# An exception path behind a flag: which block stands in front of the end, who issues its transfers, and a branch hint

## The chip, the cores and the metric

The kernel runs on one core of a Trainium2 chip. The metric is the device time of one execution in microseconds.

## What is computed

Multi-head attention, its heads put side by side, then a two-layer network with a SiLU gate. In and out are float32.

```python
# q, k, v: (8, 12, 448, 64); w_in: (768, 2048); w_out: (2048, 768)
scores = q @ k.transpose(0, 1, 3, 2) / np.sqrt(64)
scores = scores - scores.max(-1, keepdims=True)
attn = np.exp(scores)
attn = attn / (attn.sum(-1, keepdims=True) + 1e-9)
x = (attn @ v).transpose(0, 2, 1, 3).reshape(3584, 768)
h = x @ w_in
out = (h * (1.0 / (1.0 + np.exp(-h)))) @ w_out
```

## The kernel before

The program has two paths that compute the same thing. The first, `without_maximum`, leaves out the subtraction of the row maximum. It is right as long as the sums of the exponentials stay within bounds. The second, `with_maximum`, is a plain, slow version with the maximum; it is there for inputs on which the first path is not accurate, and with the inputs measured here it does not run.

**First path.** Work on attention is cut into 24 units (8 batches, 3 groups of 4 heads). GpSimd issues the loads; TensorE makes the scores, ScalarE their exponentials, VectorE the sums' inverses and the scaling; the results go to the first layer as 16-bit tiles. The second layer is computed in fast products (sums and differences of blocks, called `S` and `D`, in place of some multiplications): `product` makes them on TensorE, `take`, `add_in`, `add_out` and `take_out` bring them out of PSUM through ScalarE and VectorE into `ost` tiles, and `store` sends those to the output from SP, near the end from ScalarE too. The last product is made in two column halves (L966, 16 matmuls of 192 columns for the second). `take_half` (L1033 to L1040) copies them out, one half on VectorE (L1039), the other on ScalarE (L1037), and `store_last` issues one store of 96 KB for each (L1004), from SP and from ScalarE.

**The order** of all instructions is made by a planner: the class `Order` keeps a model time for each engine, and every operation is noted in `od.out` with the model time at which it starts. At the end the list is sorted by that time and written out, so each engine's queue follows it. `od.pe_last` is the model time at which TensorE's last operation starts.

**The flag.** `judge` (L213) runs in three steps placed some time after the last inverse sum: GpSimd compares all inverse sums with two bounds, VectorE and a small transfer reduce the answers to one number, and GpSimd writes it as an integer to `flag` (L232): 1 if the first path was good. `read_flag` (L1921) has each of the five engines load `flag` into a register with a TENSOR_LOAD (L1922). It is placed at `od.pe_last`, so behind most of the work in each queue.

**The branch.** `tc.If(fine != 1, preferred_fallthrough_block=False)` at L210 is carried out by each engine for itself, when its own queue comes to it. The argument says that the false side follows directly on the branch. There is no `Else`, so the false side holds only what the framework puts there: waits and additions that bring the semaphores to the values that they would have after the other side. In memory the order of the code is: first path, false side, true side (`with_maximum`), end block. The end block (its instructions have the line of the launch, L1956) holds SP's waits on all transfers and engines and then a barrier of the five engines. In `with_maximum` every transfer is issued by SP: the second layer's weights once, and in loops over batches and heads the loads of `q`, `k` and `v`, four small transfers of row maxima a head, the first layer's weights and the output. The arithmetic there is on TensorE, VectorE and ScalarE.

## Time and profile before

| | us |
|---|---|
| median of 3 runs | 387.40 (387.12 to 387.53) |
| the profiled execution | 386.63 |
| its span, first to last instruction | 384.84 |
| last matmul group (L966) starts | 374.13 |
| last copy (L1037) starts | 376.10, takes 0.32 |
| last store is issued (L1004, ScalarE) | 376.45 |
| granted TensorE clock | 0.995 |

In the profile's lines an engine's name with a q behind it (SPq, ACTq) is that engine's sequencer: its DMA issues, branches, semaphore waits and register loads, which are not counted as busy. PEldq stands for TensorE's sequencer. A line with "x2: 38/46/53, 376.7 to 380.3" gives how often an instruction ran, its shortest, median and longest duration in nanoseconds, and when the first and the last started. An instruction's duration does not include the time after it in which the engine has no instruction to run; that shows as the distance to the next one.

### The profile page before, as it was taken

The page shows a single profiled execution, that of the slowest core. Times are in us where ns is not written, and L with a number is a line of the kernel's source. Part 1 is how long each engine was busy: PE and PEld are TensorE (multiplying, and loading weights), DVE is VectorE, ACT ScalarE, POOL GpSimd, SP SyncE. Part 2 cuts the span into 40 slices and gives each one's busy share as a digit, 9 for nine tenths or more (in the row PEclk, how much of TensorE's full clock was granted, in tenths as well). Part 3 has the DMA queues.
Part 4 walks back from the last instruction along what each step waited for, and adds up shares of the span by engine and source line. Part 5 has one row for each costly group of instructions (what it writes and reads, how often), then busy time and mean ns, then how long its engine had stood idle before and what let it go on. Part 6 is the DMA issues. An engine that isn't in the chain of part 4 may idle for free. (4 is left out here: it accounts for less than half of the span.)

```text
span 384.8 us, 12974 instructions
## 1 busy us (share of the span) xinstructions
PE 374.1 (97%) x5516; PEld 192.6 (50%) x5516; DVE 280.8 (73%) x562; ACT 257.7 (67%) x425; POOL 91.1 (24%) x160
## 2 busy tenths in 40 slices
PE   8999999999999999999999999999999999999990
PEld 7433455444545444544444554555556555556660
DVE  5779799999978779996879897899784345473420
ACT  4998845887867787868697877558752288862220
POOL 7538517206051605142411400030020000000000
PEclk9999999999999999999999999999999999999997
DMA  7999999847367824558661712110003320002331
GB/s 116 202 204 195 189 210 193 123 87 105 64 111 145 139 43 50 82 93 157 97 115 27 97 40 68 34 33 1 2 20 84 92 52 2 1 22 67 99 97 55
DMA packets 36001, 34.74 MB, mean 90 GB/s; under 512 B 12000, under 2 KB 35168, under 8 KB 35936
## 3 DMA queue, kind: packets, MB, share of 16 engines
q0 software_dynamic: 25232, 22.82, 39.7%
q1 hardware_dynamic: 10176, 10.53, 10.2%
q8 instruction: 45, 0.74, 0.7%
q10 hardware_dynamic: 528, 0.49, 0.5%
q14 instruction: 20, 0.16, 0.1%
HBM read 45.61 MB, written 11.01 MB: 147 GB/s over the span
## 5 line engine op out<-in xcount | busy, mean ns | idle before, releaser
L608 ACT ACTIVATE E<-banks 128x896 f16<-128x896 f32 x168 | 144.0, 920 | 40.7 <-PE banks L570 40.4
L560 PE MATMUL banks<-xT,w_in_t 128*32 128x448 f16 (+1 forms) x1446 | 90.5, 353 | 0.0
L560 PE MATMUL banks<-w_out_t,G 128*32 128x384 f16 (+1 forms) x968 | 67.4, 327 | 0.0
L560 PEld LDWEIGHTS <-G 128*32 128x32 f16 (+1 forms) x1240 | 46.9, 97 | 34.0 <-issue 6.5
L560 PEld LDWEIGHTS <-w_in_t 128*32 128x32 f16 (+1 forms) x1446 | 42.2, 97 | 43.3 <-issue 12.7
L506 POOL DMA_DIRECT2D V<-in_v_dram x84 | 46.0, 555 | 57.2 <-PE banks L645 42.9
L570 PE MATMUL banks<-rq,KT 32*128 32x448 f16 (+1 forms) x768 | 52.1, 362 | 0.3 <-ACT E L608 0.2
L769 ACT ACTIVATE th<-banks 128x448 f16<-128x448 f32 x72 | 37.2, 553 | 15.0 <-PE banks L560 12.3
L807 DVE SCALAR_TENSOR_TENSOR G<-th,banks 128x448 f16<-128x448 f16 (+1 forms) x72 | 39.9, 573 | 4.8 <-ACT th L769 4.5
L1030 ACT COPY ost<-banks 128x384 f32<-128x384 f32 x41 | 19.8, 486 | 33.0 <-PE banks L560 21.4
L560 PE MATMUL banks<-D,S 128*32 128x384 f16 (+1 forms) x544 | 38.1, 327 | 0.0
L929 ACT ACTIVATE G<-banks 128x448 f16<-128x448 f32 (+3 forms) x72 | 33.8, 554 | 5.3 <-DVE banks L912 3.5
L645 PE MATMUL banks<-E,V 128*32 128x448 f16 x672 | 35.7, 353 | 0.0
L743 DVE SCALAR_TENSOR_TENSOR xT<-banks,rdn 128x448 f16<-128x448 f32 x48 | 29.2, 618 | 5.6 <-PE banks L645 3.0
L912 DVE TENSOR_TENSOR banks<-banks,q 128x448 f32<-128x448 f32 x28 | 17.6, 632 | 15.7 <-PE banks L896 14.5
L560 PEld LDWEIGHTS <-S 128*32 128x32 f16 (+1 forms) x544 | 20.6, 97 | 14.7 <-issue 3.1
L619 DVE TENSOR_TENSOR T<-E,E 128x1792 f16<-128x1792 f16 x22 | 23.8, 1081 | 5.7 <-ACT E L608 5.5
L483 POOL DMA_DIRECT2D rq<-in_q_dram x25 | 13.9, 555 | 58.4 <-PE banks L570 47.8
L619 DVE TENSOR_TENSOR T<-T,E 128x1792 f16<-128x1792 f16 x22 | 23.9, 1086 | 5.2 <-ACT E L608 5.1
L570 PEld LDWEIGHTS <-KT 32*128 32x128 f16 (+1 forms) x768 | 12.3, 96 | 29.6 <-issue 26.9
L645 PEld LDWEIGHTS <-V 128*32 128x32 f16 x672 | 17.0, 97 | 16.0 <-issue 3.9
L896 PEld LDWEIGHTS <-w_in_t 128*128 128x128 f16 x168 | 16.4, 98 | 15.2
(163 smaller groups left out, 409.4 us busy)
## 6 DMA issues: line engine op xcount, KB each, us to landing
out_dram<-ost SPq DMA_DIRECT2D x200, 48.0 KB, 1.6
rk<-in_k_dram POOLq DMA_DIRECT2D x23, 224.0 KB, 5.2
rq<-in_q_dram POOLq DMA_DIRECT2D x23, 224.0 KB, 5.1
w_out_t<-in_moe_w_out_dram POOLq DMA_DIRECT2D x4, 768.0 KB, 13.4
V<-in_v_dram POOLq DMA_DIRECT2D x42, 64.0 KB, 3.6
V<-in_v_dram POOLq DMA_DIRECT2D x42, 48.0 KB, 4.2
w_in_t<-in_moe_w_in_dram POOLq DMA_DIRECT2D x3, 512.0 KB, 10.4
w_in_t<-in_moe_w_in_dram POOLq DMA_DIRECT2D x6, 256.0 KB, 6.1
```

Source lines behind the costliest of these rows:

```text
L506: nc.gpsimd.dma_start(out=v_of(b, hg0)[32 * x : 32 * (x + 1), at, 0:count, :], in_=v[b, hs].rearrange("h (i g) d -> i h g d", g=TPP)[:, :, ...
L560: nc.tensor.matmul(out=out[at], lhsT=lhsT[:, at], rhs=rhs, **flags)
L570: nc.tensor.matmul(out=pS[p0 : p0 + 32 * (x1 - x0), h % 2, at : at + nq], lhsT=KT[(b, hg)][32 * h : 32 * (h + 1), c, x0:x1, :, e], rhs=QT[ ...
L608: nc.scalar.activation(out=E[(n, w)][0:kr, 2 * y : 2 * y + 2, 0:nk], in_=pS_t[(n, w, y)][0:kr, :, 0:nk], func=AF.Exp, scale=attn_scale,)
L619: nc.vector.tensor_tensor(out=T[n], in0=T[n] if step else E[(n, 0)], in1=E[(n, step + 1)], op=ALU.add,)
L645: nc.tensor.matmul(out=a[32 * h : 32 * (h + 1), 0:nq], lhsT=w, rhs=e[k0:k1, h, at : at + nq], start=start, stop=stop,)
L743: nc.vector.scalar_tensor_tensor(out=x3(b, cc)[:, cc % 3, 32 * g0 : 32 * g1], in0=acc[(n, part)][:, 0:nq], scalar=0.5, in1=rdn_t[n].rearra ...
L769: nc.scalar.activation(out=th, in_=h_t[(b, f, t0)][:, 0 : t1 - t0], func=AF.Tanh)
L807: nc.vector.scalar_tensor_tensor(out=dst[:, f, at + lo : at + hi], in0=th_t[(b, f, t0)][:, lo - t0 : hi - t0], scalar=1.0, in1=h_t[(b, f, ...
L912: nc.vector.tensor_tensor(out=pp_t[(f, to)], in0=pp_t[(f, x)], in1=pf_t[(f, y)], op=ALU.add)
L929: nc.scalar.activation(out=o, in_=a, func=AF.Silu, scale=2.0)
L1030: nc.scalar.copy(out=ost(qd, i, j), in_=bank(qd, m))
```

## The change

The second path's transfers are issued by GpSimd in place of SP. The flag is inverted: 0 now means that the first path was good. `with_maximum` moves from the true side of the branch to an `Else`; the true side, taken when the flag is 0, is empty. `preferred_fallthrough_block=False` stays, so the code of the false side follows on the branch and the empty true side comes behind it, in front of the end block. A new step `foretell`, placed 5 us of model time ahead of `od.pe_last`, has ScalarE, VectorE, GpSimd and SP load the flag once more and give a hint, from that register, on the branch labelled "judged". TensorE has no hint. The later load of the flag, on which the branch decides, stays where it was.

```diff
-    fine = without_maximum(tc, q, k, v, moe_w_in, moe_w_out, out, guard, flag)
-    with tc.If(fine != 1, preferred_fallthrough_block=False):
+    ran_over = without_maximum(tc, q, k, v, moe_w_in, moe_w_out, out, guard, flag)
+    with tc.If(ran_over == 0, preferred_fallthrough_block=False, label="judged") as answer:
+        pass
+    with answer.Else():
         with_maximum(tc, q, k, v, moe_w_in, moe_w_out, out)
...
-        nc.gpsimd.tensor_copy(out=flag, in_=one)
+        nc.gpsimd.tensor_scalar(
+            out=flag, in0=one, scalar1=-1.0, scalar2=1.0, op0=ALU.mult, op1=ALU.add
+        )
...
-    nc.sync.dma_start(out=w_out_t, in_=moe_w_out.rearrange("(f p) m -> p f m", p=128))
+    nc.gpsimd.dma_start(out=w_out_t, in_=moe_w_out.rearrange("(f p) m -> p f m", p=128))
...
-        nc.sync.dma_start(out=raw, in_=src[b, h].rearrange("(g i) d -> i g d", i=32))
+        nc.gpsimd.dma_start(out=raw, in_=src[b, h].rearrange("(g i) d -> i g d", i=32))
...
-            nc.sync.dma_start(out=vt, in_=v[b, h].rearrange("(c p) d -> p c d", p=112))
+            nc.gpsimd.dma_start(out=vt, in_=v[b, h].rearrange("(c p) d -> p c d", p=112))
...
-                nc.sync.dma_start(out=row[:, 112 * c : 112 * (c + 1)], in_=m)
+                nc.gpsimd.dma_start(out=row[:, 112 * c : 112 * (c + 1)], in_=m)
...
-            nc.sync.dma_start(
+            nc.gpsimd.dma_start(
                 out=w,
...
-            nc.sync.dma_start(out=out[at : at + 112], in_=o)
+            nc.gpsimd.dma_start(out=out[at : at + 112], in_=o)
...
+    def foretell():
+        some = [ENG.Activation, ENG.DVE, ENG.Pool, ENG.SP]
+        guess = nc.values_load(flag, engines=some, skip_runtime_bounds_check_because=why)
+        tc.mark_branch_hint_location("judged", guess, some)
+
+    od.out.append((od.pe_last - 5.0, len(od.out), foretell))
     od.out.append((od.pe_last, len(od.out), read_flag))
```

## The prediction

> **What bounds the kernel now.** I read the page first: where the span goes, and what is left of it when the arithmetic is over.

> ```profile
> span 384.8 us, 12974 instructions
> ...
> PE 374.1 (97%) x5516; PEld 192.6 (50%) x5516; DVE 280.8 (73%) x562; ACT 257.7 (67%) x425; POOL 91.1 (24%) x160
> ...
> PE   8999999999999999999999999999999999999990
> ```

> TensorE is busy to the last slice, and that slice is empty. The change touches nothing that feeds TensorE, so the question is the last slice. The timeline of its last ten microseconds comes next:

> ```profile
> 374.13 1.48 PE L966 MATMUL banks<-D,G 128*128 128x192 f16 x16
> ...
> 376.10 0.32 ACT L1037 COPY ost<-banks 128x192 f32<-128x192 f32 x1 [1.29 <-DVE ost L1039]
> 376.45 0.65 ACTq L1004 DMA_DIRECT2D out_dram<-ost  x1
> ```

> The last instruction that computes ends at 376.4 us and the last store is issued at 376.45; the span runs to 384.8. So 8.4 us are left with no arithmetic. What fills them are branch and semaphore instructions, which the views by source line show: line 210 (the `tc.If`) and line 1956 (the end of the program). Columns: operation, count, shortest/median/longest in ns, first and last start.

> ```profile
> L210 SPq EVENT_SEMAPHORE  x8: 17/17/17, 376.8 to 380.2; - x8
> L210 POOLq COMPARE_BRANCH  x2: 38/39/40, 287.6 to 287.7; - x2
> L210 PEldq COMPARE_BRANCH  x2: 90/2132/4173, 374.4 to 375.8; - x2
> L210 DVEq COMPARE_BRANCH  x2: 51/53/55, 375.7 to 376.2; - x2
> L210 SPq COMPARE_BRANCH  x2: 38/46/53, 376.7 to 380.3; - x2
> L210 ACTq COMPARE_BRANCH  x2: 38/50/61, 377.1 to 377.3; - x2
> ```
> ```profile
> L1956 SPq EVENT_SEMAPHORE  x14: 17/28/28, 383.2 to 384.8; - x14
> ...
> L1956 POOLq DRAIN  x3: 46/107/5792, 287.9 to 384.6; - x3
> L1956 SPq DRAIN  x3: 7/7/7, 384.0 to 384.3; - x3
> L1956 DVEq DRAIN  x2: 10/45/80, 379.3 to 384.3; - x2
> L1956 ACTq DRAIN  x2: 8/44/81, 379.9 to 384.3; - x2
> L1956 PEldq DRAIN  x2: 8/40/73, 380.0 to 384.3; - x2
> ```

> Each engine branches twice. The first branch (not taken: the flag is 1) falls into an empty block that only settles semaphores; the second jumps over all of `with_maximum` to the end block. From second branch to first instruction of the end block: DVE 376.2 to 379.3, 3.1 us; ACT 377.3 to 379.9, 2.6; PE 375.8 to 380.0, 4.2; SP 380.3 to 383.2, 2.9; POOL 287.7 to 287.9, 0.2. POOL is the control: in the code every transfer of `with_maximum` is SP's and its arithmetic is on the other three, so POOL has next to nothing to jump over. A long jump costs 2.6 to 4.2 us, a short one 0.2. Four of the five are covered, because SP still waits for the stores; SP's is not. It stands behind its eight waits of line 210, whose last are for the two output halves; issued at 376.1 and 376.45, these take 3.7 and 3.5 us and so land by 380.0. In the windows nothing else runs:

> ```profile
> 378.70:380.00 1.30, 0.00 (x0) 0.00 (x0) 0.00 (x0) 0.00 (x0) 0.00 (x0) 1.00 0.06 15
> ...
> 380.30:383.20 2.90, 0.00 (x0) 0.00 (x0) 0.00 (x0) 0.00 (x0) 0.00 (x0) 0.62 0.04 11
> ```

> The last two columns are the DMA share and GB/s. From 378.7 to 380.0 the share is 0.06, one engine of sixteen, with the last of the output on it. The DMA view from 375 to 380 names who else was there:

> ```profile
> q14 instruction: 3, 0.02, 1.6%
> q8 instruction: 1, 0.02, 1.5%
> ```

> One instruction packet of 16 KB took 1.5% of 16 x 5 us, 1.2 us on a single engine, just while the output was being written; the output packets of that engine came after it. Code is being loaded for the jumps, and it delays the landing.

> **The change part by part, on the profiled execution (386.63 us: span 384.84 and 1.79 around it; the median of the runs, 387.40, is 0.77 higher).**

> *Order of the blocks.* The false side is still the one that falls through, but it is now `with_maximum`; the true side, empty, comes behind it and runs into the end block. So each engine jumps once, at its first branch. For SP that is at 376.7, right behind its last store, in place of 380.3: the jump leaves the path behind the landing, **-2.9 us**. It lies beside the landing, which lasts to 380.0; even a full 2.9 us from 376.7 would end at 379.6.

> *Transfers from GpSimd.* SP keeps next to nothing in `with_maximum`, so its jump should cost what POOL's did, 0.2. The transfer queues of SP are also no longer used by the second path, so the empty block need not level their semaphores: the eight waits of line 210 go. Three of them stood behind the landing (the rows of SP at 380.0 to 380.3), **-0.3**. POOL gets the long jump: it branches at 287.6, 96 us before anyone asks for it; covered.

> *The end block's waits.* SP has twelve waits from 383.2 to 384.0, 0.065 us each; with the narrower window eight start by 383.64, and four and a drain follow from 383.7. The two halves' semaphores stand at the eighth and ninth. Arriving early, SP has done the first seven before the landing: 383.2 to 383.7, **-0.5**. What stays behind the landing is 383.7 to 384.84, 1.1 us.

> *The landing itself.* PE's jump, not hinted, now starts at 374.4 in place of 375.8, 1.4 us earlier; at the row's 4.2 us it is done by 378.6, and its 16 KB packet ends at about 377.3 in place of 378.7. Behind it that DMA engine has its sixteenth of the 192 KB store (the window 376.5 to 377.0 moved 0.17 MB, so 0.57 us) and of the two halves (378.7 to 379.6 before, 0.9). That gives 378.8 for the last packet where it was 379.6: **-0.8**. The bounds are 0 (another packet in the way) and -1.4 (all of the shift). The hinted engines' packets move to about 370, out of this stretch.

> *Loading the flag early and the hint.* On ACT, DVE, POOL and SP one TENSOR_LOAD, 0.48, 0.54, 0.50 and 0.97 us by the rows of line 1922, and a hint, which no row shows. Queued behind them on ACT are the copies that empty the last banks, on DVE the additions of line 1043, on SP the stores. Five microseconds ahead of the last product is about 369: there ACT idles 0.92 and 1.70 us before its copies, DVE 3.41 before line 1043, SP waits 2.7 for the copy of 370.4. Loads on the sequencer also run beside an operation (DVE's at 373.05 beside the addition at 373.03). Taken as 0, with 0.1 left for the sum. Bounds of the hint: nothing, or the 2.6 to 3.1 us of a whole fetch if it holds its queue; less than nothing is excluded, since all that it could save is the jumps, priced already. Less those idle stretches the upper end is about 1.3 us on the last copies.

> *The inverted flag.* One GpSimd operation at 285 takes the place of another (1.99 us), 80 us ahead: 0.

> Sum: -2.9 - 0.3 - 0.5 - 0.8 + 0.1 = -4.4, so 386.63 becomes 382.2, and against the median 387.4 becomes **383.0 us**. Next late after the landing (379.2) is PE, out of its jump at 378.6.

> **Rivals.**

> *The landing does not come earlier.* Another engine's code packet, or PE's own, meets the halves again. For: four packets in five microseconds, on engines I cannot choose. Against: three of them should have gone by then. Price: the 0.8 returns, 383.8. Chance 0.22.

> *The hint fetches nothing.* DVE then starts its fetch at 375.7 and ACT at 377.1, as early or earlier than before, and both are out at 378.8 and 379.7, before or at the landing; SP's short jump is untouched. Their two packets stay in the output's stretch, so the 0.8 shrinks or goes: 383.5 to 384.0. Speaking for it is that no row shows a hint. [...] Chance 0.12.

> *Nothing moves.* If the block in front of the end still closes with a jump that is not local, or SP keeps code enough in the second path for a jump behind the landing, all of 2.9 + 0.3 + 0.5 comes back: 387.4. Against: the empty block is now the neighbour of the end. Chance 0.04.

> *Slower.* [...] Chance 0.06.

> **How the numbers follow.** Forecast 0.56, the others as above. A measurement of this kernel can tell about 0.2%, 0.8 us, from no change. The first three cases are faster by more: 0.90. Nothing moves: 0.04 same. Slower: 0.06. The range goes down to the whole shift of the landing and a little run spread (387.4 - 5.1 = 382.3, so 382.0) and up past both milder rivals and the hint's upper end (383.8 + 1.3 = 385.1, so 385.0). The likeliest case alone spans 382.2 to 383.6.

> **What would show it.** Right: one branch per engine of the `tc.If`; SP's at 376.7 with the end block's first wait within about 0.3 us; no semaphore waits of SP between; the last wait of the landing followed by the end after 1.1 us; landing near 379.2; span near 380.4. PE's branch should still show some 4 us. Wrong: SP's gap of 2.9 us still behind the landing; idle time before the copies of 370 to 376 grown by more than the loads; a last copy later than 376.1; or PE's jump ending after the landing, which would make PE the last to arrive.

## The result, and the profile after

The changed kernel takes 383.88 us (median of 4 runs, 383.29 to 383.98) against 387.46 us for the kernel before (4 runs): a ratio of 0.9905, 95% interval 0.9888 to 0.9922, 3.6 us less. Its profiled execution took 383.98 us with a span of 382.2.

The spans of the two profiled executions differ by 2.7 us only. All work up to the last store is 0.9 us later in the one after (its last store is issued at 377.38, that of before at 376.45). We put that down to spread between executions and not to the change: the profiled execution of before was 0.8 us under its median, and in the profiles of the runs below, apart from the one that moves that store to SP, it is issued anywhere from 376.6 to 377.5. From the issue of the last store to the end of the span the two show 384.84 - 376.45 = 8.4 us and 382.18 - 377.38 = 4.8 us, and this difference of 3.6 us is the one of the medians. In what follows, times of the tail are counted from that issue.

The branch of the changed kernel (by source line: operation, count, shortest/median/longest ns, first and last start):

```profile
L210 PEldq COMPARE_BRANCH  x1: 3594/3594/3594, 375.4 to 375.4; - x1
L210 DVEq COMPARE_BRANCH  x1: 84/84/84, 376.7 to 376.7; - x1
L210 SPq COMPARE_BRANCH  x1: 64/64/64, 377.9 to 377.9; - x1
L210 ACTq COMPARE_BRANCH  x1: 76/76/76, 378.1 to 378.1; - x1
L210 PEldq EVENT_SEMAPHORE  x1: 51/51/51, 379.0 to 379.0; - x1
L210 DVEq EVENT_SEMAPHORE  x1: 21/21/21, 379.6 to 379.6; - x1
L210 ACTq EVENT_SEMAPHORE  x1: 17/17/17, 381.3 to 381.3; - x1
```

Each engine branches once, and SP's eight waits of this line are gone. But the long jumps are all still there: from branch to the next instruction PE 3.6 us (which its branch record itself lasts), DVE 2.9, ACT 3.2. The hints of ACT and DVE ran at 369.8 and 370.8, and no code was fetched for them: between 365 and 376 the DMA view lists no instruction packet at all. The end block and ScalarE's hint (a hint too has the line of the launch), and SP's own waits:

```profile
L1967 SPq EVENT_SEMAPHORE  x14: 17/28/28, 378.1 to 382.1; - x14
...
L1967 ACTq BRANCH_PREFETCH_HINT  x1: 54/54/54, 369.8 to 369.8; - x1
```
```profile
SPq L1967 <- ACTq L210: 1.5, 1, 1.5
SPq L1967 <- DMA out_dram<-ost: 1.1, 3, 0.4
```

SP enters the end block at 378.1, 0.2 us after its branch, in place of 383.2. It then waits 1.1 us for the output, and after that 1.5 us for ScalarE. Landing times of the last two stores (KB, us from issue):

```profile
out_dram<-ost SPq DMA_DIRECT2D x1, 96.0 KB, 2.3
out_dram<-ost ACTq DMA_DIRECT2D x1, 96.0 KB, 2.2
```

They were 3.7 and 3.5. The output is there at 379.6, when VectorE's jump ends too; after that only ScalarE's jump is outstanding, for another 1.7 us.

### The profile page after: what moved, and what is told of

Its sections match the earlier page's. It is cut to its first block, busy times and chain, and to the rows that moved or that the text cites. A ratio compares the mean times of both kernels' runs of the same rounds, so it can differ in the third digit from the quotient of the medians.

```text
span 382.2 us, 12974 instructions
## 1 busy us (share of the span) xinstructions
PE 374.5 (98%) x5516; PEld 192.9 (50%) x5516; DVE 280.9 (73%) x562; ACT 257.6 (67%) x425; POOL 91.1 (24%) x160
## 4 chain that ended last, share of the span: by engine, by line
PE 92%; ACT 2%; DMA 2%; POOL 1%; DVE 1%; issue 1%; POOLq 0%
PE banks L565 53%; PE banks L901 15%; PE banks L575 10%; PE banks L650 10%; ACT E L613 2%; DMA rq<-in_q_dram 2%; PE banks L971 2%; PE banks L666 2%; DMA out_dram<-ost 1%; POOL rk L480 0%; DVE T L624 0%; POOL rq L488 0%; PE banks L686 0%; DVE rq L558 0%; DVE ost L1053 0%
```

## Experiments

Ratios are to the kernel before on the same chip, with 95% intervals. Where source lines shift, the end block has another number (L1956, L1966 or L1967 in the lines shown).

**The hint taken away.**

```diff
-    od.out.append((od.pe_last - 5.0, len(od.out), foretell))
```

> The changed kernel without the early load and the hint. Theory (the hint fetched nothing: in the changed kernel ScalarE's jump still took 3.2 us and VectorE's 2.9): same time as the changed kernel, 383.9 us within 0.5, with ScalarE's end-block entry again the last to arrive, some 3.9 us after the last store is issued. Rival (the hint did part of the work, for instance kept the output's landing at 2.2 us): the landing goes back to 3.5 us and the time up by about 1 us.

Measured: 384.14 us, ratio 0.992 (0.9897 to 0.9942); it and the changed kernel's interval overlap over more than half of each.

```profile
L210 ACTq COMPARE_BRANCH  x1: 62/62/62, 377.6 to 377.6; - x1
L210 ACTq EVENT_SEMAPHORE  x1: 17/17/17, 380.4 to 380.4; - x1
```

ScalarE's jump takes 2.8 us without a hint and 3.2 with it, and is the last arrival in both; the landing is 2.5 us without the hint. At 5 us ahead the load and the hint gain nothing that can be measured.

**Transfers alone.** The kernel before, with only the second path's transfers moved from SP to GpSimd; its lines are numbered as before.

> The kernel before with the second path's transfers on GpSimd; order of the blocks and flag as before. Theory: SP's jump behind the landing is then local (0.2 us in place of 2.9) and its eight waits are gone; ScalarE's second branch starts 0.85 us after the last store and takes 2.6 to 3.2, so it is last: 383.6 to 384.2, nearly all of the gain without the change of order. Rival (the gain comes from the order of the blocks): 386.5 to 387.4.

Measured: 383.75 us, ratio 0.9902 (0.9885 to 0.9918), the whole gain.

```profile
L210 SPq COMPARE_BRANCH  x2: 38/46/53, 377.0 to 377.1; - x2
L210 ACTq COMPARE_BRANCH  x2: 38/50/61, 377.5 to 377.7; - x2
```
```profile
q8 instruction: 1, 0.02, 1.5%
out_dram<-ost ACTq DMA_DIRECT2D x1, 96.0 KB, 3.6
```

SP has no second jump behind the landing, nor waits between its two branches. Here TensorE still jumps late (376.2), a packet of 16 KB lies in the output (377.8; that it is TensorE's, the run without its code shows below), and the landing takes 3.6 us, beside 3.5 in the kernel before. It ends at 380.4, where ScalarE (380.5) and TensorE (380.5) come out of their jumps too. So the earlier jumps of the changed kernel bring the landing forward (2.2 us), and ScalarE's jump (3.2 us) uses that up.

**Order of the blocks alone.** The changed kernel without the hint, its second path's transfers back on SP.

> The changed kernel without the hint and with the second path's transfers back on SP: only the order of the blocks and the flag are changed. Theory: SP jumps right behind its last store, 2.9 us beside the landing, and then has its eight waits (0.5) and the twelve of the end block (0.8) to do, which the changed kernel did during the landing: SP becomes last instead of ScalarE, about 0.8 us behind it, 384.7 us; most of the gain of 3.6 is there. Rival (the gain comes from SP having no code to jump over): no gain, 387.4.

Measured: 385.1 us, ratio 0.9938 (0.9922 to 0.9955), 2.6 us gained.

```profile
L210 SPq EVENT_SEMAPHORE  x8: 17/17/17, 380.6 to 381.1; - x8
...
L210 SPq COMPARE_BRANCH  x1: 45/45/45, 377.4 to 377.4; - x1
```

SP's jump is long again, 3.2 us, but starts 0.8 us behind the last store, without waiting for the output. That output has landed at 379.2, so the jump lies beside the landing for 1.8 us and is the last thing for another 1.4. Then come the eight waits and the twelve of the end block (its drain is at 381.9), with SP still last. Either part alone thus ends the state in which SP begins its jump only when the output is there: the order lets the jump begin earlier, the transfers make it short. The gains do not add up, because both remove the same wait.

**A hint 75 us ahead**, in front of the last two code packets of queue q14 before the tail (334.3 and 351.1 us in the changed kernel).

```diff
-    od.out.append((od.pe_last - 5.0, len(od.out), foretell))
+    od.out.append((od.pe_last - 75.0, len(od.out), foretell))
```

> The changed kernel with the early load and the hint 75 us of model time ahead in place of 5, ahead of the last code packets that ScalarE and VectorE fetch in sequence (332 to 351 us). Theory A (a hint is only served together with a later fetch in sequence, so 5 us was too late): the jumps of ScalarE and VectorE shrink from 3 us to some tenths, the landing or TensorE's jump becomes last, and the time falls by about 1.5 us to 382.3. Theory B (the hint is not served in this program at any distance): 383.9, jumps of 3 us as before.

Measured: 382.81 us, ratio 0.9871 (0.9847 to 0.9894). Once more, on a chip with the changed kernel beside it:

> The hint 75 us ahead once more: 1.0 to 1.3 us below the changed kernel on the same chip (382.7), because ScalarE's jump is short and the landing and VectorE's jump, both some 2.3 us after the last store's issue, are last.

> The changed kernel once more, beside the next two on one chip: 383.9 us, a ratio of 0.990 to 0.991 to the kernel before; ScalarE's jump last, about 3.9 us after the last store's issue.

Measured there: 382.38 (382.28 to 382.84), ratio 0.9871 (0.9854 to 0.9888), against 383.10 (382.72 to 383.90), ratio 0.9892 (0.9873 to 0.9912), for the changed kernel. The step is 0.7 us, less than the 1.0 expected. The early hint came out 0.3 us under its 382.7, the changed kernel 0.8 under its 383.9. The two intervals overlap; of the runs only the slowest of the one and the fastest of the other cross. ScalarE's jump took 2.8 us in this profile of the changed kernel, 3.2 in the first. From the first run of the early hint:

```profile
L210 DVEq COMPARE_BRANCH  x1: 84/84/84, 376.7 to 376.7; - x1
...
L210 ACTq COMPARE_BRANCH  x1: 76/76/76, 378.1 to 378.1; - x1
L210 ACTq EVENT_SEMAPHORE  x1: 17/17/17, 378.6 to 378.6; - x1
...
L210 DVEq EVENT_SEMAPHORE  x1: 21/21/21, 379.8 to 379.8; - x1
```
```profile
L1967 ACTq BRANCH_PREFETCH_HINT  x1: 54/54/54, 298.6 to 298.6; - x1
L1967 DVEq BRANCH_PREFETCH_HINT  x1: 55/55/55, 299.9 to 299.9; - x1
```

ScalarE's jump takes 0.5 us; VectorE's, hinted at the same time, still 3.1, which theory A did not expect. Now VectorE (379.8) and the landing (379.6) are last. The second run shows the same: ScalarE 0.5 us, VectorE 2.9.

**A hint 15 us ahead**: the same edit with 15.0.

> The changed kernel with the load and the hint 15 us of model time ahead in place of 5: five times as long as a jump takes, but behind the last code packet that ScalarE and VectorE fetch in sequence (before 352 us). Theory A (a hint is only served together with a later fetch in sequence): ScalarE's and VectorE's jumps stay near 3 us and the time at 383.9 to 384.1. Theory B (5 us was too short a lead): ScalarE's jump falls to about 0.5 us, the time to 382.8.

Measured: 383.40 us, ratio 0.9902 (0.9886 to 0.9919), 0.5 us under the time of theory A, whose jumps came.

```profile
L210 ACTq COMPARE_BRANCH  x1: 76/76/76, 377.6 to 377.6; - x1
...
L210 ACTq EVENT_SEMAPHORE  x1: 17/17/17, 380.7 to 380.7; - x1
```
```profile
L1967 ACTq BRANCH_PREFETCH_HINT  x1: 54/54/54, 359.9 to 359.9; - x1
```

The hint of ScalarE ran at 359.9, 18 us before its branch, and its jump took 3.1 us. So a lead of 18 us, several times the length of a jump, was not enough. For ScalarE alone a longer lead, between 18 and 79 us, is not excluded; against it speaks VectorE, which was not served with a lead of 77 us.

Between 330 and 355 the DMA view counts two packets on queue q14 in this kernel, in the changed one and in the one without a hint, but one where the hint came at 299: the packet near 334 us is in all of them, the one near 351 is missing there. The trace does not say which engine a code packet is for. An estimate can be made from the instructions that each engine had begun when these packets went out, counted in the trace of this run (the trace of the changed kernel counts the same within 1): ScalarE 188, 317, 448 and 571 at the packets of 123, 199, 269 and 334 us, VectorE 320, 448 and 572 at those of 162, 229 and 289, SP 83 and 210 at those of 180 and 351. These are even steps of 123 to 131 instructions. By them, if code is fetched in its order, ScalarE's last fetch in sequence is at 334, VectorE's at 289 and not between 332 and 351 as was expected, and the packet that is missing is SP's.

**A fixed hint on all five engines.** No load; the hint says "LikelyTaken" and was placed at 120 us of model time ahead.

```diff
-        some = [ENG.Activation, ENG.DVE, ENG.Pool, ENG.SP]
-        guess = nc.values_load(flag, engines=some, skip_runtime_bounds_check_because=why)
-        tc.mark_branch_hint_location("judged", guess, some)
-
-    od.out.append((od.pe_last - 5.0, len(od.out), foretell))
+        some = [ENG.PE, ENG.Activation, ENG.DVE, ENG.Pool, ENG.SP]
+        tc.mark_branch_hint_location("judged", "LikelyTaken", some)
+
+    od.out.append((od.pe_last - 120.0, len(od.out), foretell))
```

> The changed kernel with a fixed hint (taken) in place of the one from the register, 120 us of model time ahead, on all five engines: before VectorE's fetch in sequence near 289 us, and with more than one such fetch to come on ScalarE and TensorE. [...] Theory A' (a hint stays in force until its branch): all jumps short, landing alone is last: about 382.5. Theory B (VectorE is not served at all): VectorE's jump stays at 3.

Measured: 383.07 us, ratio 0.9889 (0.9873 to 0.9906). The hints did not run where they were placed, but at the very start, at 0.7 to 0.8 us of the span. All jumps are short all the same:

```profile
L210 PEldq COMPARE_BRANCH  x1: 390/390/390, 375.2 to 375.2; - x1
...
L210 DVEq COMPARE_BRANCH  x1: 84/84/84, 376.5 to 376.5; - x1
L210 DVEq EVENT_SEMAPHORE  x1: 21/21/21, 377.1 to 377.1; - x1
L210 ACTq COMPARE_BRANCH  x1: 76/76/76, 377.9 to 377.9; - x1
...
L210 ACTq EVENT_SEMAPHORE  x1: 17/17/17, 378.4 to 378.4; - x1
```

TensorE's branch lasts 0.4 us in place of 3.6; VectorE needs 0.6 us to its next instruction, ScalarE 0.5. A fixed hint given some 375 us ahead thus still counts at its branch: theory A' for the jumps. Together with the other distances (ScalarE's jump 0.5 us with the hint at 298.6, 3.1 and 3.2 with it at 359.9 and 369.8) this fits the reading that a hint has to be there before the engine's last fetch in sequence ahead of the branch. It does not prove it, since this hint differs from the others in kind as well as in time: no run gives a register's hint to VectorE before 289 us, or a fixed one late. The time is no better than with the register's hint at 75 us: the landing is last (the half from SP takes 2.8 us, to 379.7). A 16 KB code packet still goes out at 376.3, behind TensorE's branch; that it is the reason was not tried.

**The floor.** No hint, and all of the second path but one small transfer left out.

> The changed kernel without the hint, and with all of the second path left out but one small transfer (it would give no result for inputs that need it). No engine then has a long jump and no code packet lies in the output's last stretch: this is the floor of the whole change. The landing should take 2.0 to 2.3 us from the last store's issue, followed by 1.1 us: 382.4 us. If the landing itself, not the code packets, made the 3.5 us of the kernel before, it stays at 3.5 and the time is 383.8.

Measured: 382.22 us, ratio 0.9881 (0.9861 to 0.9902); no code packet from 376 to 380.5, landing 2.1 us (ScalarE's half). It is a bound, not a kernel to use. The order at the end differs too: VectorE and ScalarE branch at 374.1 and 374.8 in it, before their last copies. The time is 4.9 us under the kernel before on the same chip. The early hint is 4.9 and 5.1 us under it on its two chips, at the floor as far as can be told; the changed kernel is 3.6 and 4.4 us under it.

**TensorE's code packet.** The kernel with the transfers alone, and VectorE's fills in place of the second path's matmuls.

> The kernel before with the second path's transfers on GpSimd (as in the run with that change alone), and in the second path VectorE's fills in place of its matmuls (it would give no result). TensorE's jump is then short and its 16 KB code packet gone. Theory (that packet held back the last output on one DMA engine): the landing falls from 3.6 us to about 2.5 from the last store's issue; ScalarE's jump, 3.6 us behind the store, stays last, so the time moves little, 383.4 to 383.8. Rival (the packet plays no part): landing 3.6.

Measured: 383.45 us, ratio 0.9901 (0.9884 to 0.9917).

```profile
out_dram<-ost ACTq DMA_DIRECT2D x1, 96.0 KB, 2.5
```

The landing falls from 3.6 to 2.5 us when that packet is gone, and the time hardly moves, since ScalarE leaves its jump (380.8) after the landing (380.0).

**The last store from SP**, so that ScalarE can branch during its copy.

```diff
-        store_last(1, 0, h, nc.scalar if x else nc.sync)
+        store_last(1, 0, h)
```

> The changed kernel with the last store issued from SP in place of ScalarE. ScalarE can then branch while its last copy runs, 0.7 to 1.0 us earlier. If ScalarE's jump is what ends the changed kernel, the time falls by 0.7 us, to 383.2; the last store is issued some 0.5 us later and its landing (2.2 us) comes to about the same moment as ScalarE's entry, so no more than that. If something else is last, no change or 0.5 us slower.

Measured: 383.07 us, ratio 0.9886 (0.9867 to 0.9904), beside 383.10 of the changed kernel: no gain.

```profile
L210 ACTq COMPARE_BRANCH  x1: 68/68/68, 376.8 to 376.8; - x1
...
L210 ACTq EVENT_SEMAPHORE  x1: 17/17/17, 379.6 to 379.6; - x1
```

ScalarE branches as its copy starts (376.8) and is out of the jump 2.7 us later, at 379.6. But SP issues the second half only at 378.0, its first issue having taken 1.1 us; that landing is last, at 380.0. The expected 0.7 us did not come: a new wait took the place of the old one. The run shows that ScalarE can be taken off the path in this way, and that it does not pay here.

## Why the prediction was right, and where it was not

*The range and the sign were right; the likeliest case was not the one that came.* 383.88 lies outside that case's own range (382.2 to 383.6) and inside the 383.5 to 384.0 of the rival "the hint fetches nothing", which had a chance of 0.12. That rival had the hint right, but its number fits in part by luck: it let the landing come late and ScalarE before it, where the landing came early and ScalarE late.

*SP's jump, its waits and the end block (-2.9, -0.3, -0.5).* Right. SP went from branch to end block in 0.2 us, as POOL's row had it, and did its first waits during the landing. The experiments split this: the order of the blocks alone gives 2.6 us, the transfers alone 3.9. So the 2.9 us that the prediction books under the order are not all the order's: alone, it leaves SP's jump last, 1.4 us behind the landing, where the prediction let even a full jump end before it.

*The landing (-0.8).* Right in cause, too small in size: 3.5 became 2.2 us, 1.3 less. The run without TensorE's second-path code shows the cause by itself (3.6 to 2.5 us). But nothing of this gain reached the end.

*"Next late after the landing is PE."* This is the step that failed, and it failed through the one on the hint. The hint was counted as fetching: ScalarE's and VectorE's packets were to move to about 370. No packet moved. ScalarE's jump then lasted to 3.9 us behind the last store, 1.7 behind the landing. The rival that said so took ScalarE's jump from the row of before, 2.6 us, and let it end before the landing; it took 3.2, so ScalarE took the place of SP. With the landing this early 2.6 us would have been too long as well: in the second run of the changed kernel the jump took 2.8, and SP still waited 0.8 us for ScalarE. The forecast had the last arrival 2.7 us after the last store (3.5 - 0.8); it came after 3.9, 1.2 later. What follows it took 0.9 us in place of 1.1, because ScalarE's semaphore is the last that SP waits for. The sum without its allowance, -4.5, becomes -4.5 + 1.2 - 0.2 = -3.5, beside -3.6 measured.

*The loads and the hint at no cost.* Right: with and without them the times agree (ratios of 0.9905 and 0.992 to the kernel before), and the hint itself takes 0.05 us.

## What to carry to other kernels

Code that never runs cost time here because the end lay behind it (2.9 us for SP's jump in the kernel before): look at what the queue does after the last store, engine by engine, and put the jump ahead of the last wait or give that engine nothing to jump over; here either alone gave most of the gain or all of it. When one engine's jump leaves the path, look at the others' at once, since they were hidden only by the one removed (here ScalarE's, 3.2 us). A branch hint earned nothing here by standing 5 or 15 us ahead (ScalarE's jump 3.2 and 3.1 us, 2.8 without a hint). These runs fit, and do not prove, that it has to be given before the engine's last fetch of code in sequence (ScalarE: hinted at 298.6, last fetch estimated at 334, jump 0.5 us); if so, a hint behind that fetch comes too late (VectorE: hinted at 299.9, last fetch estimated at 289, jump 3.1 us), and an engine that has made its last fetch before the flag exists can't be served by the flag.
